# A fixed order of issue for the attention front of a lightning-attention and low-rank mixer kernel, with weight conversion in smaller steps

## Chip, cores and metric

The kernel runs on one core of one Trainium2 chip. The metric is the device time of one execution in microseconds (us). All runs told here fell in the fast state and gave correct results. TensorE is the matrix engine; VectorE (DVE), ScalarE (ACT) and GpSimd (POOL) are the others that compute; SyncE (SP) issues most transfers. PEld in a profile is TensorE loading weights. The *granted clock* is the share of full speed at which TensorE was let run; "half clock" means that its instructions take about twice their usual time.

## The reference, cut to what matters

```python
# attention: B, H, S, D = 4, 8, 768, 64; blocks of 64 along S, with a decay lam per head
for b in range(nb):
    intra = einsum(einsum(qb, kb) * Dmask, vb)
    inter = einsum(qb * lam_pow, kv_state)
    out[block] = intra + inter
    kv_state = lam_block * kv_state + einsum(kb * rev_pow, vb)
x = out.transpose(0, 2, 1, 3).reshape(B, S, 512)
# mixer: U 768x32, V 32x768, w_ch1 512x2048, w_ch2 2048x512
h  = x.transpose(0, 2, 1) @ U @ V
u  = x + h.transpose(0, 2, 1)
out = u + relu(u @ w_ch1) @ w_ch2
```

U, V, w_ch1 and w_ch2 reach the kernel as 64-bit floats. It has to convert them itself.

## The kernel before

The program has two parts. The *front*, about 175 us, does attention in 24 chunks of 128 rows (4 batches of 6 chunks), the low-rank part, and the conversion of U, V and the first blocks of w_ch1. The *feed-forward*, 540 us of matmuls, follows. For each chunk `s` the front runs these pieces:

- `prep`: TensorE transposes q and k (tiles pq, pk), ScalarE copies them out (qt, kt), GpSimd makes scaled ones (qs, ks).
- `scores`: 16 matmuls (pss); VectorE multiplies them by the mask (sm).
- `outputs`: px from sm, v and the state; then the state itself (pkv, kvc, kv).
- `back`: transposes to natural rows (pxn, x_nat).
- `low`, `low_sum`: once per batch, x against U (pp, then pt), summed over four groups (pr), split in two parts (pt_h, p_hl inside vp).
- `mix`, `turn`: x plus the low-rank part (pu, x_nat), transposed and split for the feed-forward (put, ut, u_hl, te, u_d).

```python
def prep(s):
    ...                                   # 8 transposes into pq, pk
    nc.scalar.copy(qt, pq)
    nc.scalar.copy(kt, pk)
    ...                                   # GpSimd: ks, qs

def low(b, chunks):                       # called with chunks 0..4, later with chunk 5
    if 0 in chunks:
        pts[b] = bank([P, C], "pp")
    pp = pts[b]
    for c in chunks:
        g = c % G                         # G = 4 groups of 32 columns of the array
        nc.tensor.matmul(out=pp[g * R : (g + 1) * R, :], lhsT=u_w[:, c, :],
                         rhs=xs[b * NT + c], start=(c < G), stop=(c + G >= NT))
    if NT - 1 in chunks:
        pts[b] = tmp("pt")
        nc.scalar.copy(pts[b], pp)

# order of the pieces
pieces = [("prep", 0), ("scores", 0)]
for s in range(NS):
    b, c = divmod(s, NT)
    step = [("prep", s + 1)] * (s + 1 < NS)
    if b > 0:
        if c > 0:
            step += [("mix", s - NT - 1)]
        else:
            step += [("mix", s - NT - 1)] * (b > 1) + [("low_b", b - 1)]
    step += [("outputs", s)]
    step += [("scores", s + 1)] * (s + 1 < NS)
    step += [("low_a", b)] * (c == NT - 1)
    step += [("low_sum", b - 1)] * (c == 0 and b > 0)
    step += [("back", s)]
    ...                                   # turn
```

A converted weight takes these steps, hung on chunks by number:

```python
fetch  # the words, by SyncE
one    # DVE sc, DVE m; then ScalarE twice over sc
two    # DVE m, DVE sc, DVE wf (the 32-bit weight)
three  # DVE wt; ScalarE w[0]; DVE wl; ScalarE w[1]; DVE w[2]   (the split)

for steps, at in (
    (u_side, (0, 1, 1)), (v_steps(0), (0, 2, 2, 3)), (v_steps(1), (1, 4, 4, 5)),
    (w1_steps(0), (3, 8, 9, 10)), (w1_steps(1), (10, 14, 15, 16)),
): ...
```

The third block of w_ch1, `w1_steps(2)`, belongs to the code *after* the front. In the kernel before, a scheduler decides the order of everything on each engine.

Of the kernel before, what the change touches and what calls it, by code (L numbers as in the profile page):

```python
# [18 lines left out]
def kernel(  # L19
# [76 lines left out]
    def weight_steps(dst, src, n):  # L96

        st = {}
        dims = "p (c f) -> p c f" if len(src.shape) == 3 else None

        def shape(t, f):
            return t.rearrange(dims, f=f) if dims else t

        def fetch():
            if src.dtype == FP32:
                nc.sync.dma_start(out=shape(dst(), src.shape[-1]), in_=src)
                return
            words_pool.append(words_pool.pop(0))
            words = words_pool[-1].tile([P, 2 * C], U32, tag="words", name="words")[:, 0 : 2 * n]
            s = src.bitcast(U32)  # L110
            nc.sync.dma_start(out=shape(words, s.shape[-1]), in_=s)
            st["w"] = words.rearrange("p (n two) -> p n two", two=2)

        def one():
            if src.dtype == FP32:
                return
            hi = st["w"][:, :, 1]
            st["sc"] = sc = wconv.tile([P, C], U32, tag="sc", name="sc")[:, 0:n]
            st["m"] = m = wconv.tile([P, C], U32, tag="m", name="m")[:, 0:n]
            sc_f = sc.bitcast(FP32)  # L120
            nc.vector.tensor_scalar(sc, hi, 20, 0x7FF, ALU.logical_shift_right, ALU.bitwise_and)
            nc.vector.tensor_scalar(m, hi, 0xFFFFF, 0x100000, ALU.bitwise_and, ALU.bitwise_or)

            nc.scalar.activation(out=sc_f, in_=sc, func=AF.Relu, bias=ends[-1][:, 0:1], scale=-1.0)
            nc.scalar.activation(
                out=sc, in_=sc_f, func=AF.Relu, bias=ends[-1][:, 1:2], scale=-float(1 << 23)
            )

        def two():
            if src.dtype == FP32:  # L130
                return
            lo, hi = st["w"][:, :, 0], st["w"][:, :, 1]
            sc, m = st["sc"], st["m"]
            m_f, sc_f = m.bitcast(FP32), sc.bitcast(FP32)
            nc.vector.scalar_tensor_tensor(m_f, lo, 2.0**-32, m, ALU.mult, ALU.add)
            nc.vector.scalar_tensor_tensor(sc, hi, 0x80000000, sc, ALU.bitwise_and, ALU.bitwise_or)
            nc.vector.scalar_tensor_tensor(dst(), m_f, 2.0**-20, sc_f, ALU.mult, ALU.mult)

        return [fetch, one, two]

    def split_steps(tile_of, src):

        st = {}

        def dst():
            if "w" not in st:
                st["w"] = wconv.tile([P, C], FP32, tag="wf", name="wf")
            return st["w"]

        def three():  # L150
            w, t, low = st["w"], tmp("wt"), tmp("wl")
            o = tile_of()
            nc.vector.tensor_scalar(t.bitcast(U32), w.bitcast(U32), HI, None, ALU.bitwise_and)
            nc.scalar.copy(o[:, 0, :], t)
            nc.vector.tensor_tensor(out=low, in0=w, in1=t, op=ALU.subtract)
            nc.scalar.mul(o[:, 1, :], low, 4096.0)
            nc.vector.scalar_tensor_tensor(o[:, 2, :], t, -E, low, ALU.mult, ALU.add)

        return weight_steps(dst, src, C) + [three]

    w1v, w2v = {}, {}

# [18 lines left out]
    def bank(shape, name):  # L181
        return ps.tile(shape, FP32, tag="bank", name=name)
# [2 lines left out]

    raw = {}

    def load(name, s):
        b, c = divmod(s, NT)
        t = raw_pool.tile(  # L190
            [P, H, D], FP32, tag=f"{name}raw", bufs=3, name=f"{name}raw"
        )
        source = {"q": q, "k": k, "v": v}[name]
        nc.sync.dma_start(
            out=t, in_=source[b, :, c * P : (c + 1) * P, :].rearrange("h p d -> p h d")
        )
        raw[s, name] = t
# [36 lines left out]
        nc.vector.tensor_copy(out=rev, in_=mask[:, :, :, P - 1])  # L234
        nc.gpsimd.memset(kv, 0.0)

    def more_constants():
        nc.vector.memset(zeros, 0.0)
        for x in range(2):
            nc.vector.tensor_copy(  # L240
                out=lamh[x * D : (x + 1) * D, :], in_=lamb[x * D : (x + 1) * D, x::2]
            )
        for a in range(HP):
            nc.vector.tensor_tensor_scan(
                powq[:, a, :], lamh[:, a : a + 1].broadcast_to([P, P]),
                zeros.broadcast_to([P, P]), 1.0, ALU.mult, ALU.add,
            )
        grid = ident.rearrange("p (g r) -> p r g", r=R)
        nc.vector.tensor_reduce(out=gather[:, 0, :], in_=grid, axis=mybir.AxisListType.X, op=ALU.add)
        for g in range(1, G):  # L250
            nc.vector.tensor_copy(out=gather[:, g, :], in_=gather[:, 0, :])
# [108 lines left out]

    pts = {}

    def low(b, chunks):

        if 0 in chunks:
            pts[b] = bank([P, C], "pp")
        pp = pts[b]
        for c in chunks:
            g = c % G
            nc.tensor.matmul(  # L370
                out=pp[g * R : (g + 1) * R, :], lhsT=u_w[:, c, :], rhs=xs[b * NT + c],
                start=(c < G), stop=(c + G >= NT),
            )
        if NT - 1 in chunks:
            pts[b] = tmp("pt")
            nc.scalar.copy(pts[b], pp)

    def low_sum(b):
        pr = bank([P, C], "pr")
# [56 lines left out]
    for s in range(NS):  # L436
        b, c = divmod(s, NT)
        step = [("prep", s + 1)] * (s + 1 < NS)
        if b > 0:
            if c > 0:  # L440
                step += [("mix", s - NT - 1)]
            else:
                step += [("mix", s - NT - 1)] * (b > 1) + [("low_b", b - 1)]
        step += [("outputs", s)]
        step += [("scores", s + 1)] * (s + 1 < NS)
        step += [("low_a", b)] * (c == NT - 1)
        step += [("low_sum", b - 1)] * (c == 0 and b > 0)
        step += [("back", s)]
        done = s - NT - 1
        if done >= 0 and done // TG < FG:  # L450
# [1 line left out]
        pieces += step  # L452
    waiting = {name: list(range(NS)) for name in "qkv"}

    def load_next(name):
        if waiting[name]:
            load(name, waiting[name].pop(0))


    run = {  # L460
        "prep": prep, "scores": scores, "outputs": outputs, "back": back,
        "low_a": lambda b: low(b, range(NT - 1)), "low_b": lambda b: low(b, [NT - 1]),
        "low_sum": low_sum, "mix": mix, "turn": turn,
    }
    def v_steps(half):
        cols = slice(half * SH, (half + 1) * SH)
# [4 lines left out]
                st["v"] = tmp("vf")[:, 0:SH]  # L471
            return st["v"]

        def three():
            vf, t = st["v"], tmp("vt")[:, 0:SH]
            nc.vector.tensor_scalar(t.bitcast(U32), vf.bitcast(U32), HI, None, ALU.bitwise_and)
            for g in range(G):
                rows = slice(g * R, (g + 1) * R)
                if g % 2 == 0:
                    nc.scalar.copy(v_hl[rows, cols], t[rows])  # L480
                else:
                    nc.vector.tensor_tensor(
                        out=v_hl[rows, cols], in0=vf[rows], in1=t[rows], op=ALU.subtract
                    )

        return weight_steps(dst, moe_V[:, cols].unsqueeze(0).broadcast_to([G, R, SH]), SH) + [three]


    u_side = weight_steps(
        lambda: u_w.rearrange("p c r -> p (c r)"), moe_U.rearrange("(c p) r -> p c r", p=P), NT * R  # L490
    )
    side = {}
    for steps, at in (
        (u_side, (0, 1, 1)),
        (v_steps(0), (0, 2, 2, 3)),
        (v_steps(1), (1, 4, 4, 5)),
        (w1_steps(0), (3, 8, 9, 10)),
        (w1_steps(1), (10, 14, 15, 16)),
    ):
        for step, n in zip(steps, at):  # L500
            side.setdefault(n, []).append(step)

    load_next("q")
    nc.sync.dma_start(out=lamb, in_=lam.unsqueeze(0).broadcast_to([P, H]))
    load_next("k")
    load_next("v")
    for name in "qkv":
        load_next(name)
    constants()
    for i, (what, s) in enumerate(pieces):  # L510
        run[what](s)
        if i == 1:
            for name in "qkv":
                load_next(name)
            more_constants()
        if what == "scores":
            for step in side.pop(s - 1, ()):
                step()
    assert not side
    att_ctx.close()  # L520
    words_pool[:] = [wconv]

# [68 lines left out]
    def run_units(units, side, every=lambda i: None):  # L591
# [6 lines left out]

    c0, b = NS - NT, B - 1
    rest = [  # L600
        (0, 0, "mix", c0 - 1), (0, 1, "turn", c0 - 2), (0, 5, "low_b", b), (0, 10, "low_sum", b),
        (0, 18, "mix", c0), (1, 0, "turn", c0 - 1), (1, 2, "mix", c0 + 1), (1, 8, "turn", c0),
        (1, 12, "mix", c0 + 2), (1, 16, "turn", c0 + 1), (1, 20, "mix", c0 + 3),
        (2, 0, "turn", c0 + 2), (2, 4, "mix", c0 + 4), (2, 8, "turn", c0 + 3),
# [49 lines left out]
    us = {}  # L654
    acc = {}

    def product(i, n):
        g, ft = steps[i]
        m, hl, dd = ms[i], w2hl[ft // 4][:, ft % 4], w2dd[ft // 4][:, ft % 4]
        if ft == 0:  # L660
# [1 line left out]
        pz, pd = acc[n]  # L662
        cols = slice(n * P, (n + 1) * P)
        first, end = ft == 0, ft == FT - 1
        nc.tensor.matmul(out=pz, lhsT=m[:, 0, cols], rhs=hl[:, 0], start=first, stop=False)  # L665
        nc.tensor.matmul(out=pz, lhsT=m[:, 1, cols], rhs=hl[:, 1], start=False, stop=end)  # L666
        nc.tensor.matmul(out=pd, lhsT=m[:, 2, cols], rhs=dd, start=first, stop=end)  # L667

    def residual(g):

# [54 lines left out]
            for n in range(TG):  # L725
                finish(g, n)
    for n in range(TG):
        for i in range(len(steps) - STAG, len(steps)):
            product(i, n)
        finish(NG - 1, n)  # L730


# [28 lines left out]
```

## Time and profile before

| | before |
|---|---|
| time, median of 3 runs | 717.14 us (716.25 to 717.36) |
| span of the profiled execution | 714.7 us |
| TensorE busy | 97% |
| scores of chunk 23 start at | 156.6 us |
| from there to the end | 558.1 us |

The span is shorter than the time by about 2 us in every run. The starts of pss are the front's clock: a full chunk without waits takes 5.58 us, and whatever lies above that is a wait, a slower clock, or the low-rank part. A *beat* is the time from one chunk's start to the next.

Two places are not shown in the prediction and are needed later. The first is the end of the program. VectorE's timeline of the kernel before (start, length, engine, line, operation, tiles, shapes, count, and idle time with its releaser in brackets):

```profile
710.06 0.69 DVE L682 SCALAR_TENSOR_TENSOR o<-pz,u 128x512 f32<-128x512 f32 x1 [0.63 <-PE pz L666]
710.86 0.69 DVE L685 SCALAR_TENSOR_TENSOR o<-pd,o 128x512 f32<-128x512 f32 x1
```

TensorE's last matmul starts at 709.79, and VectorE ends 1.76 us after that start.

The second is the low-rank product at the second boundary of batches, in TensorE's timeline of the kernel before:

```profile
87.05 1.90 PE L370 MATMUL pp<-x_nat,u_w 128*32 128x512 f32 x10
91.01 1.04 PE L370 MATMUL pp<-x_nat,u_w 128*32 128x512 f32 x2
```

Ten passes (five chunks, two passes each) cost 1.90 us, and the two passes of the sixth chunk, issued apart, cost 1.04 us more.

### The profile page before, as it was taken

The page shows a single profiled execution, that of the slowest core. Times are in us where ns is not written, and L with a number is a line of the kernel's source. Part 1 is how long each engine was busy: PE and PEld are TensorE (multiplying, and loading weights), DVE is VectorE, ACT ScalarE, POOL GpSimd, SP SyncE. Part 2 cuts the span into 40 slices and gives each one's busy share as a digit, 9 for nine tenths or more (in the row PEclk, how much of TensorE's full clock was granted, in tenths as well). Part 3 has the DMA queues.
Part 4 walks back from the last instruction along what each step waited for, and adds up shares of the span by engine and source line. Part 5 has one row for each costly group of instructions (what it writes and reads, how often), then busy time and mean ns, then how long its engine had stood idle before and what let it go on. Part 6 is the DMA issues. An engine that isn't in the chain of part 4 may idle for free.

```text
span 714.7 us, 11406 instructions
## 1 busy us (share of the span) xinstructions
PE 695.1 (97%) x4176; PEld 561.0 (78%) x4176; DVE 506.4 (71%) x909; ACT 309.3 (43%) x543; POOL 110.5 (15%) x91
## 2 busy tenths in 40 slices
PE   6889999999999999999999999999999999999997
PEld 5768788796888888888888888888888888888885
DVE  4676868676899976667779525678677686775864
ACT  3566677575566544454546412223232232222320
POOL 3224455443300000000000000003030030300300
PEclk9999999999999999999999999999999999999999
DMA  9687967513477655565556799965335363363431
GB/s 191 143 191 162 226 153 176 148 61 133 163 242 262 230 206 208 198 214 193 191 213 244 272 326 310 383 216 200 103 119 192 89 206 103 118 188 92 163 90 59
DMA packets 131808, 131.77 MB, mean 184 GB/s; under 512 B 81320, under 2 KB 89512, under 8 KB 131752
## 3 DMA queue, kind: packets, MB, share of 16 engines
q1 hardware_dynamic: 131752, 131.04, 59.1%
q8 instruction: 33, 0.54, 0.3%
q14 instruction: 23, 0.19, 0.1%
HBM read 80.68 MB, written 50.33 MB: 183 GB/s over the span
## 4 chain that ended last, share of the span: by engine, by line
PE 90%; DVE 4%; DMA 4%; ACT 1%; issue 1%; SPq 0%; DVEq 0%; ACTq 0%
PE pz L546 25%; PE pz L666 13%; PE pz L665 13%; PE pd L553 13%; PE pd L667 13%; PE pss L293 3%; DMA words<-in_moe_V_dram 3%; PE px L316 2%; PE px L311 2%; PE pp L370 2%; PE pxn L356 1%; PE put L411 1%; PE pkv L332 1%; PE pk L263 1%; PE pq L263 1%; DMA words<-in_moe_w_ch_dram 1%
## 5 line engine op out<-in xcount | busy, mean ns | idle before, releaser
L546 PE MATMUL pz<-u_hl,w 128*128 128x512 f32 x768 | 190.0, 398 | 0.0
L546 PEld LDWEIGHTS pz<-u_hl,w 128*128 128x128 f32 x768 | 144.2, 188 | 35.9 <-issue 1.3
L667 PE MATMUL pd<-w_d,m 128*128 128x512 f32 x384 | 152.2, 396 | 0.0
L665 PE MATMUL pz<-w_hl,m 128*128 128x512 f32 x384 | 152.2, 396 | 0.0
L666 PE MATMUL pz<-w_hl,m 128*128 128x512 f32 x384 | 152.2, 396 | 0.0
L650 ACT ACTIVATE m<-mt 128x512 fp32r<-128x512 f32 x96 | 60.7, 632 | 192.2 <-PE pd L667 145.0
L651 DVE SCALAR_TENSOR_TENSOR m<-rm,m 128x512 fp32r<-128x512 f32 x96 | 71.5, 746 | 49.4 <-ACT m L650 49.1
L561 DVE SCALAR_TENSOR_TENSOR r<-pd,r 128x512 f32<-128x512 f32 x96 | 61.9, 685 | 59.0 <-ACT r L560 51.0
L687 POOL TENSOR_TENSOR o<-o,u 128x512 f32<-128x512 f32 x20 | 29.8, 1521 | 449.9 <-DVE o L685 449.9
L553 PE MATMUL pd<-u_d,w 128*128 128x512 f32 x384 | 98.4, 397 | 0.0
L560 ACT ACTIVATE r<-pz 128x512 f32<-128x512 f32 x96 | 52.3, 596 | 99.4 <-PE pz L546 99.4
L666 PEld LDWEIGHTS pz<-w_hl,m 128*128 128x128 f32 x384 | 72.3, 188 | 17.6
L667 PEld LDWEIGHTS pd<-w_d,m 128*128 128x128 f32 x384 | 72.3, 188 | 17.6
L665 PEld LDWEIGHTS pz<-w_hl,m 128*128 128x128 f32 x384 | 72.3, 188 | 17.6
L553 PEld LDWEIGHTS pd<-u_d,w 128*128 128x128 f32 x384 | 72.1, 188 | 17.3
L652 DVE SCALAR_TENSOR_TENSOR m<-m 128x512 fp32r<-128x512 f32 x96 | 68.7, 717 | 0.9
L649 DVE TENSOR_SCALAR mt<-rm 128x512 uint32<-128x512 uint32 x96 | 46.2, 481 | 27.9 <-DMA rm<-r_d 27.6
L316 PE MATMUL px<-sm,vraw 128*64 128x128 f32 x384 | 41.3, 285 | 3.5 <-DVE sm L299 3.4
L311 PE MATMUL px<-qs,kv 128*64 128x128 f32 x320 | 37.2, 285 | 1.5 <-issue 1.5
L316 PEld LDWEIGHTS px<-sm,vraw 128*64 128x64 f32 x384 | 29.7, 143 | 8.6 <-DVE sm L299 5.7
L299 DVE TENSOR_TENSOR sm<-pss,mask 128x512 f32<-128x512 f32 x48 | 30.9, 684 | 7.3 <-PE pss L293 6.1
L280 POOL TENSOR_TENSOR qs<-qt,powq 128x512 f32<-128x512 f32 x20 | 26.5, 1324 | 55.5 <-ACT qt L267 55.5
(81 smaller groups left out, 774.2 us busy)
## 6 DMA issues: line engine op xcount, KB each, us to landing
r_d<-r SPq DMA_DIRECT2D x96, 256.0 KB, 2.1
rm<-r_d SPq DMA_DIRECT2D x96, 256.0 KB, 2.7
words<-in_moe_w_ch_dram SPq DMA_DIRECT2D x32, 512.0 KB, 4.1
w_d<-w SPq DMA_DIRECT2D x16, 768.0 KB, 3.3
w_hl<-w_d SPq DMA_DIRECT2D x16, 512.0 KB, 6.3
qraw<-in_q_dram SPq DMA_DIRECT2D x24, 256.0 KB, 4.1
kraw<-in_k_dram SPq DMA_DIRECT2D x24, 256.0 KB, 4.9
vraw<-in_v_dram SPq DMA_DIRECT2D x24, 256.0 KB, 4.0
```

The source lines that it names most:

```text
L311: nc.tensor.matmul(out=px[rows, a, :], lhsT=kv[:, a, rows], rhs=qs[:, a, :], start=True, stop=False,)
L316: nc.tensor.matmul(out=px[x * D : (x + 1) * D, a, :], lhsT=vr[:, 2 * a + x, :], rhs=sm[:, x, a, :], start=(c == 0), stop=True,)
L546: nc.tensor.matmul(out=acc[g][0], lhsT=w[:, n, ct, :], rhs=uhl[g][:, n, ct, :], start=(ct == 0 and n == 0), stop=(ct == CT - 1 and n == 1),)
L553: nc.tensor.matmul(out=acc[g][1], lhsT=w[:, 2, ct, :], rhs=ud[g][:, ct, :], start=(ct == 0), stop=(ct == CT - 1),)
L560: nc.scalar.mul(r, pz, 1.0 + E)
L561: nc.vector.scalar_tensor_tensor(r, pd, 4096.0, r, ALU.mult, ALU.add)
L650: nc.scalar.activation(out=m[:, 0], in_=t, func=AF.Relu)
L651: nc.vector.scalar_tensor_tensor(m[:, 1], r, 0.0, hi, ALU.max, ALU.subtract)
L652: nc.vector.scalar_tensor_tensor(m[:, 2], hi, E, low, ALU.mult, ALU.subtract)
L665: nc.tensor.matmul(out=pz, lhsT=m[:, 0, cols], rhs=hl[:, 0], start=first, stop=False)
L666: nc.tensor.matmul(out=pz, lhsT=m[:, 1, cols], rhs=hl[:, 1], start=False, stop=end)
L667: nc.tensor.matmul(out=pd, lhsT=m[:, 2, cols], rhs=dd, start=first, stop=end)
```

## The change

The intent: the scheduler lets VectorE start on words that have not landed, while a score product waits. So fix the order of issue for the whole front, cut the conversion into smaller steps at chosen places, and bring the low-rank product together.

```diff
-        return [fetch, one, two]
+        return [fetch, one, two, three]       # two and three: the old two, halved
-    def low(b, chunks):
+    def low(b):
-        for c in chunks:
+        for c in range(NT):
...
+        step += [("mix", s - NT - 1)] * (s > NT)
+        step += [("low", b - 1)] * (c == 0 and b > 0)
         step += [("outputs", s)]
+        step += [("low_sum", b - 1)] * (c == 0 and b > 0)
         step += [("scores", s + 1)] * (s + 1 < NS)
-        step += [("low_a", b)] * (c == NT - 1)
-        step += [("low_sum", b - 1)] * (c == 0 and b > 0)
         step += [("back", s)]
...
-        (u_side, (0, 1, 1)),
-        (v_steps(0), (0, 2, 2, 3)),
-        (v_steps(1), (1, 4, 4, 5)),
-        (w1_steps(0), (3, 8, 9, 10)),
-        (w1_steps(1), (10, 14, 15, 16)),
+        (u_side, (None, -2, 2, 2)),
+        (v_steps(0), (None, -3, 4, 4, 5, 5)),
+        (v_steps(1), (3, -5, 5, 6, 6, -7)),
+        (w1_steps(0), (7, -9, 10, 11, 12)),
+        (w1_steps(1), (9, -14, 15, 16, 17)),
...
+    with tc.manual_schedule():
+        load_next("q")
+        load_next("k", nc.scalar)
+        nc.scalar.dma_start(out=lamb, in_=lam.unsqueeze(0).broadcast_to([P, H]))
+        for name in "vqkvqkv":
+            load_next(name)
+        for step in first:                    # None: words of U and V, ahead of the front
+            step()
+        constants()
+        for i, (what, s) in enumerate(pieces):
+            run[what](s)
...
+            if what == "outputs":
+                for step in early.pop(s, ()): # negative numbers: behind outputs(|n|)
+                    step()
+            if i + 1 == len(pieces) or pieces[i + 1][0] == "prep":
...
+                for step in late.pop(n, ()):  # positive numbers: at the end of chunk n
+                    step()
...
     for n in range(TG):
-        for i in range(len(steps) - STAG, len(steps)):
-            product(i, n)
+        for parts in ((0, 1), (2,)):          # last sums: pz of three steps, then pd
+            for i in range(len(steps) - STAG, len(steps)):
+                product(i, n, parts)
         finish(NG - 1, n)
```

V's steps are now six (the split has two parts). The code behind the front, with `w1_steps(2)`, is still ordered by the scheduler. Line numbers move: pss is L293 before and L302 after, kt L268 and L277, pp L370 and L377.

> **What bounds the kernel now.** I read the page first, then the chain of waits in order of time, then TensorE's timeline for its gaps, and the timelines of the engines that it waited for.
>
> ```profile
> PE 695.1 (97%) x4176; PEld 561.0 (78%) x4176; DVE 506.4 (71%) x909; ACT 309.3 (43%) x543; POOL 110.5 (15%) x91
> ```
>
> TensorE is the bound, and most of that can't move. The two feed-forward products are 1152 + 1152 matmuls of 512 columns (the page's L546, L553, L665, L666, L667), and the chain shows eight of them in 1.87 to 1.88 us, so 0.234 us each and 540 us in all. Of the 714.7 us span, 175 us are left for the attention front, the start and the end. The change works there. The front has 24 chunks, and the starts of their score matmuls (pss) give its beat.
>
> ```profile
> 14.17 1.09 PE pss L293 x16
> 17.65 18.19 DMA words<-in_moe_V_dram x2
> 47.39 1.09 PE pss L293 x16
> 106.65 1.09 PE pss L293 x16
> 112.24 1.14 PE pss L293 x16
> ```
>
> These are lines of the chain: start, length, work. Between 106.65 and 112.24 a chunk takes 5.59 us and TensorE has no gap: the pace of a full chunk. In the first batch, which has no mixing yet, TensorE's timeline has starts at 14.10, 19.02 and 23.93: 4.92 us. But chunks 1 to 6 take 33.2 us (14.17 to 47.39), where five times 4.92 is 24.6. The next view, TensorE's timeline, has the gaps.
>
> ```profile
> 37.15 1.07 PE L316 MATMUL px<-sm,vraw 128*64 128x128 f32 x3 [1.98 <-DVE sm L299]
> 98.24 0.47 PE L394 MATMUL pu<-vp 128*128 128x512 f32 x1 [0.80 <-DVE vp L387]
> 124.75 1.16 PE L293 MATMUL pss<-qt,kt 64*128 64x128 f32 x16 [0.72 <-ACT kt L268]
> ```
>
> The bracket is idle time and who ended it. VectorE's own timeline says why sm was late:
>
> ```profile
> 35.87 0.36 DVE L121 TENSOR_SCALAR sc<-words 128x384 uint32<-128x384 uint32 x1 [2.05 <-DMA words<-in_moe_V_dram]
> 36.14 0.35 DVE L122 TENSOR_SCALAR m<-words 128x384 uint32<-128x384 uint32 x1
> 36.41 1.28 DVE L299 TENSOR_TENSOR sm<-pss,mask 128x512 f32<-128x512 f32 x2
> ```
>
> The masked scores stand in VectorE's queue behind a conversion whose words have not landed.
>
> **What the Trainium skill says.** (1) "TensorE: Matmul & The Clock Gate", the opening table: ScalarE's, VectorE's and GpSimd's queues are strict FIFO. The trace agrees: sm above waited 2.05 us for data that is not its own. So the order of issue alone can cost or win time. (2) The same page, "What's actually happening": the array falls to half clock when idle and comes back after sustained work. The trace agrees: after the 1.98 us gap the granted clock of 35 to 40 us is 0.73. A stall can cost more than its own length. (3) "GPSIMD Engine Reference", Specifications: its SBUF interface is shared with VectorE, with contention for instructions with two SBUF inputs. The trace agrees: wl (two SBUF inputs) takes 1.58 us at both of its places in the front, beside running GpSimd work, against a median of 0.686 over its 32 runs of the same size. (4) "DMA: Bandwidth & Descriptors", "Issuing engines are not separate DMA queues": a second issuing engine saves issue time only. So k0 on ScalarE's queue gains at most its later issue (1.85 instead of 0.74 us), shared with q0's transfer.
>
> **The change, part by part.** I take TensorE's pace without gaps and add the waits that the new order makes.
>
> *Start.* pss of chunk 0 began at 7.97. k0 goes out about 1.1 us sooner, but q0 still needs its four transposes at half clock (1.09 us), then k0's (1.1), then kt (0.59). VectorE used to finish masks, powers and gather before sm, at 10.09; now powers (1.37) and gather (0.34 + 1.23) come later, so it is free. I gain 0.7 us: chunk 1 at 13.4.
>
> *First batch.* Words are fetched early and converted behind the scores. Five beats of 4.92: chunk 6 at 38.0. I add 0.5 for raw loads that now queue behind 0.6 MB of words. Before: 47.3. Gain here 8.8 beyond none, with the start included.
>
> *Low-rank part.* All twelve passes (1.83 + 0.97 = 2.80 us) and the gather product (1.05) now come ahead of the next scores, so their results ripen behind 3.0 us of other TensorE work (1.09 + 0.58 + 0.44 + 0.88), where 1.5 are needed. A batch's boundary of two chunks becomes 8.56 + 5.58 = 14.14 us; before it took 15.05 twice. Gain 0.9 at each before new waits. At the first boundary 7.9 + 5.3 = 13.2 against 14.1.
>
> *Two chunks each at 72.6 to 86.0 and 112.2 to 124.75.* These lose 1.2 + 1.5 and 1.9 us today to words and to conversion in front of sm. Without waits they take 5.58 and, for a last chunk without state, 5.12.
>
> *Sum without new waits:* 13.4 + 24.6 + 13.2 + 3 x 5.58 + 5.12 + 14.14 + 3 x 5.58 + 5.12 + 14.14 + 3 x 5.58 = 139.9 us for the start of chunk 23's scores, against 156.6 now: 16.7 us of gain at most.
>
> *New waits.* The fixed order puts ScalarE's two writes of a converted weight ahead of the next chunk's qt and kt, where the scheduler had slipped kt in front. These are lines of before for one such conversion, VectorE's and ScalarE's:
>
> ```profile
> 117.22 1.58 DVE L155 TENSOR_TENSOR wl<-wf,wt 128x512 f32<-128x512 f32 x1
> 116.55 0.57 ACT L268 COPY kt<-pk 128x512 f32<-128x512 f32 x1
> 118.83 0.63 ACT L156 ACTIVATE w<-wl 128x512 fp32r<-128x512 f32 x1 [0.58 <-DVE wl L155]
> ```
>
> There ScalarE waits for wl after kt; in the new order kt waits with it. At the second boundary, from the end of the gather product: VectorE does pt_h and p_hl (1.45), sm (1.25), ut and u_hl (1.4), wt (0.5), wl (1.58): 6.2. Then ScalarE's w (0.63) and qt, kt (1.05): 7.9. TensorE wants kt at 5.6 (one beat). Wait 2.3 us. By the same count at the third boundary (no pt_h, one step of another weight between, then the copy pt): 7.85 against 6.42, 1.4 us. At chunk 8, V's second half: vf at 1.5, its writes, then kt: 0.9 to 1.8, I take 1.3. The two opening steps add 1.45 us of ScalarE work (two of 0.72) ahead of kt, which has about 1.05 of room in a beat: 0.4 each. With the 0.5 of the loads: 6.3 us.
>
> *End.* The last pz sum now ends three matmuls before pd, so L682 (0.69) runs beside pd, instead of between 710.06 and 710.86: about 0.5 us off. Nothing else in the 540 us moves.
>
> Total: 16.7 - 6.3 + 0.5 = 10.9, so 706.2. Some of the counted waits may not fall so badly, since VectorE's contention is the largest guess in them, so I say 705.5.
>
> **The rivals.** *All waits gone:* the steps fit in VectorE's and ScalarE's slack, wl is not slowed. For it: a beat without conversion leaves VectorE 1.37 us idle before kvc. Against it: wl took 1.58 both times. Time: 717.1 - 17.2 = 699.9. *ScalarE becomes the wait:* as I count, with the 2.3 us gap bringing half clock again as at 37 us, 1.7 us more: about 708. *Loads become the wait:* the transfers ran full from 5 to 20 us (218 GB/s); words of U and V put ahead of chunks 3 and 4's q and k could delay them by their 0.6 MB, 2.7 us. Up to chunk 3's q and k there are eleven pieces of 0.262 MB and 0.59 MB of words, 3.47 MB in all; with 0.58 MB moved in the first 5 us (116 GB/s) and 218 to 223 GB/s after it, they are in by about 18.2, wanted at about 19: thin. If they miss: 2 us more and perhaps half clock, 708 to 710. *The scheduler was better:* a fixed order that blocks at every chunk would give back everything, 715 or more; the unchanged beat of 5.58, which the scheduler reached with the same order of scores, output and state, speaks against it.
>
> **Range and chances.** The ends are 699.9 (no new wait) and about 710 (mine plus clock and loads). 2% faster means under 702.8, a gain of 14.3 out of 17.2 possible: new waits would have to stay under 2.9 us, where I count 6.3. I give that 0.3, within 2% 0.67, slower 0.03. Range 700.0 to 710.5.
>
> **What would show it.** Right: pss starts 4.92 apart from chunk 1 to 6, no wait of VectorE for words, chunk 6 near 38; low-rank boundaries without pu waiting for vp; TensorE's longest gap at chunk 14's pss, waiting for ScalarE's kt, about 2.3 us, with wl at 1.58 and w ahead of kt; smaller ones at chunks 8 and 19; L682 of the last rows ended before the last matmul. Wrong: q or k as releaser of TensorE at 18 to 25 us, wl at 0.7 us, kt never a releaser, or a beat other than 5.58 in chunks without conversion.

## The result

| | before | after |
|---|---|---|
| time, median of 4 runs | 717.05 us (716.25 to 717.36) | 712.22 us (711.04 to 713.1) |
| span of the profiled execution | 714.7 us | 710.8 us |
| scores of chunk 23 start at | 156.6 us | 153.4 us |
| from there to the end | 558.1 us | 557.4 us |

The ratio is 0.9933, 95% interval 0.9916 to 0.9951. Ratios here are the mean time of one kernel's fast runs over that of the other's fast runs of the same rounds, so not quite the ratio of the medians that are quoted. The change is faster by 0.7%, which counts as "within 2%". The predicted 705.5 us was 6.7 us too low; the range had ended at 710.5.

Part 1 of the page after, with busy time by engine:

```profile
PE 690.2 (97%) x4176; PEld 560.0 (79%) x4176; DVE 508.2 (71%) x909; ACT 308.5 (43%) x543; POOL 109.9 (15%) x91
```

The number of instructions per engine is the same as before, so only their order and grouping differ. Next, TensorE's timeline of the kernel after, cut to the larger gaps and what follows the largest:

```profile
21.31 0.66 PE L272 MATMUL pq<-ident,qraw 128*128 128x128 f32 x4 [0.70 <-DMA qraw<-in_q_dram]
22.51 0.63 PE L272 MATMUL pk<-ident,kraw 128*128 128x128 f32 x4 [0.55 <-DMA kraw<-in_k_dram]
45.27 1.05 PE L377 MATMUL pp<-x_nat,u_w 128*32 128x512 f32 x2 [1.07 <-ACT x_nat L367]
55.52 1.16 PE L302 MATMUL pss<-qt,kt 64*128 64x128 f32 x16 [1.37 <-ACT kt L277]
73.80 1.16 PE L302 MATMUL pss<-qt,kt 64*128 64x128 f32 x16 [0.54 <-ACT kt L277]
93.72 1.16 PE L302 MATMUL pss<-qt,kt 64*128 64x128 f32 x16 [1.38 <-ACT kt L277]
106.13 1.16 PE L302 MATMUL pss<-qt,kt 64*128 64x128 f32 x16 [0.53 <-ACT kt L277]
127.11 2.07 PE L386 MATMUL pr<-pt,gather 128*128 128x512 f32 x2 [3.48 <-DVE kvc L348]
129.11 2.08 PE L302 MATMUL pss<-qt,kt 64*128 64x128 f32 x16
```

TensorE's 1.98 us wait for sm of the kernel before is gone. In its place stand waits for ScalarE's kt, foreseen, and one of 3.48 us at the third boundary of batches, not foreseen in this size. The two lines at the end take about twice their usual 1.13 and 1.16 us: half clock.

The starts of pss give a ledger by stretch of chunks. "Predicted" adds up the prediction's terms for the stretch. The last two columns are two experiments told below.

| stretch | predicted | after | third weight fixed | best |
|---|---|---|---|---|
| start to chunk 1 | 13.4 | 13.9 | 13.9 | 12.4 |
| 1 to 6 | 25.1 | 25.8 | 25.9 | 24.9 |
| 6 to 8 (first boundary, V) | 14.5 | 15.8 | 15.8 | 13.1 |
| 8 to 12 | 22.3 | 23.6 | 23.6 | 24.2 |
| 12 to 14 (second boundary) | 16.4 | 14.6 | 14.6 | 13.3 |
| 14 to 18 | 22.3 | 23.3 | 23.3 | 23.6 |
| 18 to 20 (third boundary) | 15.5 | 19.6 | 14.1 | 13.3 |
| 20 to 23 | 16.7 | 16.8 | 18.0 | 18.4 |
| chunk 23 starts at | 146.2 | 153.4 | 149.0 | 143.2 |

Each column is one execution. The changed kernel's second profiled execution (told below) took 12.6, 29.9 and 13.6 us in the first three stretches, 56.1 us in all where the first took 55.5, and agreed within 0.1 us from chunk 8 on; so the split of the first three rows is loose.

The kernel after misses the prediction by 7.1 us at chunk 23, and 4.1 of them lie in one stretch, from 18 to 20. Four views of the kernel after show that place. First VectorE's timeline:

```profile
119.61 0.67 DVE L421 TENSOR_SCALAR ut<-put 128x512 uint32<-128x512 uint32 x1
120.70 0.43 DVE L121 TENSOR_SCALAR sc<-words 128x512 uint32<-128x512 uint32 x1 [0.42 <-DMA words<-in_moe_w_ch_dram]
121.05 0.68 DVE L431 TENSOR_TENSOR u_hl<-put,ut 128x512 fp32r<-128x512 f32 x1
121.98 1.51 DVE L122 TENSOR_SCALAR m<-words 128x512 uint32<-128x512 uint32 x1
123.41 1.54 DVE L162 TENSOR_TENSOR wl<-wf,wt 128x512 f32<-128x512 f32 x1
```

L121 and L122 here are step `one` of the *third* weight. They come from the code behind the front, and the scheduler has put them into VectorE's queue inside the fixed stretch, between the instructions of chunk 18 (ut and u_hl are the turn of chunk 11, which is done there). L121 waits for words, u_hl waits behind it, and L122 and wl take 1.51 and 1.54 us, where 0.42 and 0.69 are their usual lengths (L122 took 1.50 us at 68.30 and at 100.64 too). The chain of waits of the kernel after runs through the transfer of those words:

```profile
116.14 4.46 DMA words<-in_moe_w_ch_dram
```

Then ScalarE's timeline:

```profile
124.98 0.63 ACT L163 ACTIVATE w<-wl 128x512 fp32r<-128x512 f32 x1 [2.27 <-DVE wl L162]
125.98 0.59 ACT L277 COPY kt<-pk 128x512 f32<-128x512 f32 x1
126.46 0.60 ACT L382 COPY pt<-pp 128x512 f32<-128x512 f32 x1
```

ScalarE idles 2.27 us for wl, and only after that write come qt, kt and pt. pr needs pt, which ends at 127.06; TensorE starts it at 127.11. (The bracket of pr names kvc, which ended at 127.09, only 0.03 us after pt. But pr does not need it: in the run with the third weight placed by hand, told below, pr starts at 124.33, after pt's end at 124.28 and before kvc starts at 124.37.) Last the table by windows, with busy us and instructions of PE, PEld, DVE, ACT, POOL, then TensorE's granted clock, DMA share and GB/s:

```profile
120.00:125.00 5.00, 3.63 (x46) 1.81 (x44) 4.58 (x7) 1.79 (x4) 2.53 (x2) 1.00 0.89 208
125.00:130.00 5.00, 2.89 (x10) 1.39 (x12) 2.83 (x6) 3.28 (x8) 1.27 (x1) 0.64 0.66 157
130.00:135.00 5.00, 5.00 (x43) 4.53 (x43) 3.77 (x6) 2.30 (x5) 0.00 (x0) 0.68 0.03 9
```

The clock falls to 0.64 and 0.68 in the two windows. Between 130 and 135 TensorE is busy all the time and gets through 43 instructions.

The places that went better than predicted: at the second boundary wl took its normal time, and the twelve low-rank passes together took less. VectorE's and then TensorE's timeline of the kernel after:

```profile
91.35 0.69 DVE L162 TENSOR_TENSOR wl<-wf,wt 128x512 f32<-128x512 f32 x1 [0.16 <-ACT te L433]
```

```profile
82.30 1.91 PE L377 MATMUL pp<-x_nat,u_w 128*32 128x512 f32 x12
```

Twelve passes cost 1.91 us, against 1.90 + 1.04 for ten and two. The prediction had carried the old sum over.

### The profile page after: what moved, and what is told of

The parts are those of the page before. It is cut to its first block, busy times and chain, and to the rows that moved or that the text cites. A ratio compares the mean times of both kernels' runs of the same rounds, so it can differ in the third digit from the quotient of the medians.

```text
span 710.8 us, 11432 instructions
## 1 busy us (share of the span) xinstructions
PE 690.2 (97%) x4176; PEld 560.0 (79%) x4176; DVE 508.2 (71%) x909; ACT 308.5 (43%) x543; POOL 109.9 (15%) x91
## 4 chain that ended last, share of the span: by engine, by line
PE 89%; DMA 4%; DVE 4%; ACT 2%; issue 1%; SPq 0%; DVEq 0%; ACTq 0%
PE pz L561 25%; PE pz L683 13%; PE pz L681 13%; PE pd L568 13%; PE pd L685 13%; PE pss L302 3%; PE px L325 2%; PE px L320 2%; DMA kraw<-in_k_dram 1%; DMA words<-in_moe_V_dram 1%; PE pxn L365 1%; PE put L417 1%; PE pk L272 1%; PE pq L272 1%; DVE sm L308 1%
## 5 line engine op out<-in xcount | busy, mean ns | idle before, releaser
L325 PE MATMUL px<-sm,vraw 128*64 128x128 f32 x384 | 37.7, 280 | 0.3 <-DVE sm L308 0.3
L302 PE MATMUL pss<-qt,kt 64*128 64x128 f32 x384 | 29.7, 297 | 4.9 <-ACT kt L277 4.7
L302 PEld LDWEIGHTS pss<-qt,kt 64*128 64x128 f32 x384 | 24.9, 199 | 10.5 <-ACT kt L277 6.5
L320 PE MATMUL px<-qs,kv 128*64 128x128 f32 x320 | 32.9, 279 | 0.0
```

What stands on the lines that cost most here:

```text
L302: nc.tensor.matmul(out=pss[x][:, a, :], lhsT=kt[rows, a, :], rhs=qt[rows, a, :], start=True, stop=True,)
L325: nc.tensor.matmul(out=px[x * D : (x + 1) * D, a, :], lhsT=vr[:, 2 * a + x, :], rhs=sm[:, x, a, :], start=(c == 0), stop=True,)
```

## The experiments

The question has two parts: why the third boundary costs 4 us more than reckoned, and what the other parts of the change are worth. For the boundary there were three theories. *Stray steps:* the third weight's steps, which the fixed order does not hold, delay VectorE. *Writes in front:* ScalarE's two writes of a converted weight stand ahead of the next chunk's qt, kt and pt, so TensorE inherits every delay of wl. *Words:* V's and the weights' words come too late, or the chunks' loads do. Experiments are told in the order in which they answer this. "After" names the changed kernel; diffs are against it unless said otherwise. Each ratio is against the kernel before, run on the same chip.

### The third weight's steps placed by hand

```diff
+    third = w1_steps(2)
...
         (w1_steps(1), (9, -14, 15, 16, 17)),
+        (third[:3], (12, -20, 23)),
...
-    run_units([(pairs[2], 0), (pairs[2], 1)], w1_steps(2))
+    run_units([(pairs[2], 0), (pairs[2], 1)], third[3:])
```

> The changed kernel, with the third weight's fetch and first two steps given fixed places (chunks 12, 20 and 23) instead of being lifted by the scheduler into chunk 18; its last steps stay where the feed-forward part had them, so that part is not starved as it was with everything fixed. Theory C (the stray steps make the 3.48 us wait and the half clock behind it): as in the front of the all-fixed run, the wait at the third boundary is near 0.7 us, no half clock, and now the whole kernel gains it: about 5 us, 707 to 708 us. Rival (what the front gains, the feed-forward part loses to the later third and fourth weight): no better than the changed kernel, 712 us.

Measured: 708.49 us (707.96 to 708.98), ratio 0.9893 (0.988 to 0.9907), span 707.1. TensorE's timeline and two windows of this run, at the third boundary:

```profile
124.33 1.13 PE L386 MATMUL pr<-pt,gather 128*128 128x512 f32 x2 [0.72 <-ACT pt L382]
```

```profile
120.00:125.00 5.00, 4.28 (x48) 2.11 (x46) 4.55 (x7) 4.43 (x9) 3.48 (x3) 1.00 0.89 207
125.00:130.00 5.00, 5.00 (x61) 4.25 (x61) 4.41 (x7) 2.96 (x7) 1.00 (x1) 1.00 0.80 191
```

With the stray steps elsewhere wl takes 0.69 us and ends at 122.16 instead of 124.95; pr waits 0.72 us, not 3.48, and the clock stays at 1.00. The stretch from 18 to 20 takes 14.1 us, not 19.6, and the stretches before it stay as they were (ledger, the column of this run). Later a kt wait of 0.53 us appears, and 1.2 us of the gain go in chunks 20 to 23. The stray steps are shown as the cause of the large miss: 3.7 us of span, and 3.7 us of the median time.

### The writes of the weights one chunk later

```diff
-            nc.scalar.copy(o[:, 0, :], t)          # out of step four
-            nc.scalar.mul(o[:, 1, :], low, 4096.0)
+        def writes():                              # a step of its own
+            nc.scalar.copy(o[:, 0, :], t)
+            nc.scalar.mul(o[:, 1, :], low, 4096.0)
...
-        (w1_steps(0), (7, -9, 10, 11, 12)),
-        (w1_steps(1), (9, -14, 15, 16, 17)),
+        (w1_steps(0, True), (7, -9, 10, 11, 12, -13)),
+        (w1_steps(1, True), (9, -14, 15, 16, 17, -18)),
```

> The changed kernel with one thing undone: ScalarE's two writes of a converted weight (w1 of step 0 and 1) are issued one chunk later, behind the next qt, kt (and pt). Theory A (ScalarE's fixed order is what costs: kt and pt wait behind w, which waits for VectorE's wl): the 1.38 us wait for kt at 93.7 us and the 3.48 us wait at 127.1 us shrink to under 1.5 us together, the half clock after the second one is gone, about 706 us. Rival B (VectorE is behind at these places anyway, ScalarE only passes its delay on): the waits move to the scores' sm or to pu and the time stays within 2 us of the changed kernel, 710 to 712 us.

Measured: 708.74 us (708.39 to 709.13), ratio 0.989 (0.9869 to 0.9911), span 706.6. TensorE's timeline of this run at the third boundary, with the stray steps still in VectorE's queue:

```profile
122.64 1.12 PE L397 MATMUL pr<-pt,gather 128*128 128x512 f32 x2
126.73 0.63 PE L428 MATMUL put<-ident,x_nat 128*128 128x128 f32 x4 [1.30 <-DVE x_nat L414]
129.49 0.49 PE L411 MATMUL pu<-vp 128*128 128x512 f32 x1 [1.25 <-ACT vp L403]
```

VectorE is as late as in the kernel after: L122 takes 1.51, wl 1.54 us. But pt is now ahead of the writes on ScalarE, and pr has no wait. VectorE's delay reaches TensorE later and in two parts, 2.55 us in all, without half clock. So it took both for the large loss: the stray steps made wl late, and the write in front of kt and pt passed that on in one piece, with half clock behind it. The stretch from 18 to 20 takes 19.6 us with both, 16.5 with the stray steps alone, 14.1 with the writes in front alone, and 13.7 with neither (the next run).

### Both, with V's writes later too

```diff
+    third = w1_steps(2)                            # and third[:3] at (12, -20, 23), as above
-        (v_steps(0), (None, -3, 4, 4, 5, 5)),
-        (v_steps(1), (3, -5, 5, 6, 6, -7)),
+        (v_steps(0), (None, -3, 4, 4, 5, -6, -6)), # V's ScalarE writes a step of their own
+        (v_steps(1), (3, -5, 5, 6, 6, -7, -7)),
+        (w1_steps(0, True), (7, -9, 10, 11, 12, -13)),
+        (w1_steps(1, True), (9, -14, 15, 16, 17, -18)),
```

> The run with the third weight at fixed places (708.5 us), with ScalarE's writes of V's halves and of the two weights issued behind the next chunk's qt and kt. Theory A: the waits for kt at 55.5 and 93.7 us (1.37 + 1.38 us) and the 0.72 us for pt at 124.3 go; about 1.2 us come back as new waits for kt one chunk later (writes are 1.24 us, room about 0.65): 1.5 to 2.5 us faster, 706.5 us. Rival B (VectorE's backlog is the limit): 708 us or more, waits for sm, x_nat or pu in their place.

Measured: 708.43 us (707.83 to 709.47), ratio 0.9893 (0.9878 to 0.9909). It is no faster than either alone. The kt waits at 55.5 and 93.7 us and the pr wait are gone, but new ones stand at 61.95 (0.54 us) and 100.24 (1.17 us), one chunk later, as the expectation had reckoned (writes of 1.24 us, room for about 0.65). In the profiled execution q also came 2.01 us late at 21.4 us; it came 2.08 late in the run with late writes alone, and 0.74 in the one with the third weight alone. So part of the gain may be hidden by that late load. But moving the writes as a block did move the waits.

### Everything fixed, up to the first feed-forward units

```diff
+    with tc.manual_schedule():
         for i, (pair, ft) in enumerate([(pairs[0], 0), (pairs[1], 0), (pairs[0], 1), (pairs[1], 1)]):
             ...
         run_units([(pairs[2], 0), (pairs[2], 1)], w1_steps(2))
```

> The changed kernel with the first twelve feed-forward units in a fixed order too, so that the scheduler can no longer lift the third weight's first steps (L121, L122, L133) into VectorE's queue at chunk 18. Theory C (these stray steps, their wait for words and the contended 1.5 us ones make the third boundary's wait): the 3.48 us wait falls to about 1.4 us, too short for half clock, so about 5 us are won: 707 us. Rival A alone (kt and pt behind w and wl, stray steps or not): the wait stays at 2.5 us or more with half clock behind it, 711 us or more. The fixed units themselves may cost or win 1 us.

Measured: 720.22 us (719.84 to 720.86), ratio 1.0049 (1.0031 to 1.0067), span 719.0. TensorE's timeline of this run:

```profile
124.95 1.13 PE L386 MATMUL pr<-pt,gather 128*128 128x512 f32 x2 [0.72 <-ACT pt L382]
206.21 6.48 PE L561 MATMUL pz<-u_hl,w 128*128 128x512 f32 x16 [6.95 <-ACT w L161]
```

The front did what the stray-steps theory says: pr waits 0.72 us and chunk 23 starts at 148.4. But the third weight was then fetched and converted only where the code has it, and the feed-forward stood still for 6.95 us, with half clock behind it (6.48 us for 16 matmuls that take 3.91 elsewhere). The stray steps were not an error of the scheduler as such: it had filled a need that the fixed order did not know.

### The low-rank part alone, in the kernel before

Against the kernel before:

```diff
-                step += [("mix", s - NT - 1)] * (b > 1) + [("low_b", b - 1)]
+                step += [("mix", s - NT - 1)] * (b > 1) + [("low", b - 1)]   # all six chunks
-        step += [("low_a", b)] * (c == NT - 1)
```

> The kernel before with one part of the change alone: all six chunks of the low-rank product issued together, the scheduler's order otherwise. In the trace after, the twelve passes took 1.84 us (82.4 to 84.2) where the five and the one took 1.83 + 0.97 us. Theory D (issued together, chunks 4 and 5 run side by side in other columns of the array): 0.95 us less in each of four batches, 3.5 to 4 us faster than before, about 713.3 us. Rival: the passes cost the same and only the place differs: within 1 us of before, 717 us.

Measured: 713.75 us (712.81 to 714.55), ratio 0.9957 (0.9937 to 0.9978), span 711.0. Chunk 23 starts at 153.1 instead of 156.6. TensorE's timeline:

```profile
87.64 1.91 PE L368 MATMUL pp<-x_nat,u_w 128*32 128x512 f32 x12
```

Here, too, twelve passes take 1.91 us. Chunks 4 and 5 use two different groups of array columns (0 and 1); the passes of chunk 5 add nothing when they are issued beside those of chunk 4, and 1.0 us when they are issued apart. At four boundaries this is 4 x 1.0 us at most. The profiled span falls by 3.7, about as much as for the whole change (3.9); but this was the fastest of the four runs. By the means of all runs of the same rounds, the low-rank part alone is worth 2.9 us and the whole change 4.8 and 4.5 us (two rounds), with intervals that overlap. So this small part gives about two thirds of the gain. In the kernel after, the passes stayed apart at the first boundary (ten, then two, at 45.27 above).

### The last sums alone, in the kernel before

```diff
-        for i in range(len(steps) - STAG, len(steps)):
-            product(i, n)
+        for parts in ((0, 1), (2,)):
+            for i in range(len(steps) - STAG, len(steps)):
+                product(i, n, parts)
```

> The kernel before with the last sums' order alone: VectorE's next to last instruction runs beside the last three matmuls. Theory: 0.45 to 0.5 us less, 716.5 us against 717.0, the end of VectorE's last instruction 1.3 us after the last matmul's start instead of 1.76. Rival: nothing, hidden by the last transfer.

Measured: 716.21 us (714.25 to 717.86, 6 runs), ratio 1.0003 (0.9987 to 1.0019). Half a microsecond is below what these runs resolve. The trace of this run shows the mechanism all the same, VectorE ending 1.28 us after the last matmul's start, and so does that of the kernel after. VectorE's timeline of the kernel after, at its end:

```profile
706.19 0.69 DVE L700 SCALAR_TENSOR_TENSOR o<-pz,u 128x512 f32<-128x512 f32 x1 [0.61 <-PE pz L683]
706.99 0.69 DVE L703 SCALAR_TENSOR_TENSOR o<-pd,o 128x512 f32<-128x512 f32 x1
```

VectorE ends 1.29 us after TensorE's last matmul starts (at about 706.4), where the kernel before needed 1.76. L700 begins before that last start, but does not end before it.

### The first k back on SyncE's queue

```diff
-        load_next("k", nc.scalar)
-        nc.scalar.dma_start(out=lamb, in_=lam.unsqueeze(0).broadcast_to([P, H]))
+        nc.sync.dma_start(out=lamb, in_=lam.unsqueeze(0).broadcast_to([P, H]))
+        load_next("k")
```

> The changed kernel with the first k load and lambda back on SyncE's queue, in the order of before. Theory: q0 lands at 4.0 instead of 4.8 us and lambda at 4.4 instead of 6.7, k0 later; scores of chunk 0 begin within 0.5 us of the changed kernel's 7.38; the time is within 0.6 us of the changed kernel's. Rival: the early k0 is worth its 1.1 us, this run is 1 us slower.

Measured: 710.54 us (709.67 to 712.2, 6 runs), ratio 0.9921 (0.9907 to 0.9936); the interval overlaps that of the kernel after. q's transposes start at 3.96 instead of 4.77 us, and the first scores at 7.71 instead of 7.38: what k gains, q loses. This part is worth nothing that can be measured. TensorE's timeline of this run has something else to note:

```profile
21.63 0.66 PE L272 MATMUL pq<-ident,qraw 128*128 128x128 f32 x4 [1.18 <-DMA qraw<-in_q_dram]
22.82 0.64 PE L272 MATMUL pk<-ident,kraw 128*128 128x128 f32 x4 [0.54 <-DMA kraw<-in_k_dram]
23.88 0.64 PE L325 MATMUL px<-sm,vraw 128*64 128x128 f32 x4
```

From 23.4 us on px takes 0.64 us instead of 0.39 and the granted clock of 20 to 25 and of 25 to 30 us is 0.83, though no single wait was longer than 1.18 us.

### V's second half later

```diff
-        (v_steps(1), (3, -5, 5, 6, 6, -7)),
+        (v_steps(1), (3, -7, 7, 8, 8, -9)),
```

> The changed kernel with the second half of V converted two chunks later (it is first needed by the fourth mixed chunk), its words fetched at the same place. Theory E (VectorE's 3.76 us wait for V's words at 43.1 us delays x_nat, pt and then kt on ScalarE, and these cost TensorE 1.07 + 1.37 us and the unpacked passes): these waits go, new ones of about 0.5 us come at chunks 8 to 10, 1.5 to 2.5 us faster than the changed kernel, about 710 us. Rival: the wait only moves with the conversion, no gain: 712 us.

This tests the loss at chunks 6 to 8. In the kernel after, VectorE idles 3.76 us at 43.08 for V's words, which were issued at 33.45 and took 9.5 us to land.

Measured: 712.46 us (710.58 to 717.04), ratio 0.9949 (0.991 to 0.9988): no gain. The waits at 45 and 55 us are gone, but chunk 10's scores now wait 3.72 us for kt (at 66.88): on ScalarE the writes of V stand in front of kt, and they waited 2.93 us for VectorE, where two instructions of V's conversion had slowed to 1.66 and 1.03 us. Again the wait was moved and not removed.

### The words of U and V behind the chunks' loads

With the third weight placed as above, and:

```diff
-        (u_side, (None, -2, 2, 2)),
-        (v_steps(0), (None, -3, 4, 4, 5, 5)),
+        (u_side, (0, -3, 3, 3)),
+        (v_steps(0), (1, -4, 4, 4, 5, 5)),
```

> The run with the third weight at fixed places (708.5 us), with the words of U and of V's first half fetched behind the raw loads of chunks 3 and 4 and U's steps one chunk later. Loads theory (words put ahead delay q and k of chunk 3): the waits of 0.7 and 0.55 us for q and k at 21 and 22.5 us go, chunks 1 to 5 start 4.92 us apart, 1.3 to 1.7 us faster: 706.9 us. Rival: the words then come late for their conversion, VectorE waits for them and the scores behind it: no gain, 708.5 us.

Measured: 710.64 us (708.64 to 712.29, 6 runs), ratio 0.9924 (0.9908 to 0.994): slower than with the words in front. The chunks' loads are in time (chunks 1 to 5 start 4.91 us apart), but V's second half now lands later still. VectorE's and TensorE's timelines of this run:

```profile
43.58 0.36 DVE L121 TENSOR_SCALAR sc<-words 128x384 uint32<-128x384 uint32 x1 [5.85 <-DMA words<-in_moe_V_dram]
```

```profile
45.76 1.91 PE L377 MATMUL pp<-x_nat,u_w 128*32 128x512 f32 x2 [3.38 <-ACT x_nat L367]
```

VectorE waits 5.85 us with its queue blocked, TensorE 3.38 us, and the two passes take 1.91 instead of 1.05 us, at half clock. In these two orders, whichever load was put later came late.

### The changed kernel again

> The changed kernel itself again, as the base for the others on this chip: 711 to 713 us, ratio to before 0.992 to 0.995.

Measured: 712.28 us (708.78 to 713.28, 6 runs), ratio 0.9938 (0.9919 to 0.9958). This profiled execution had a wait of 2.35 us for q at 21.61 us, with half clock behind it, where the first one had 0.70 and none; the kernel before had no wait for q after the start. So the change also brought a load that comes just in time or just too late, and the spread of 4.5 us is wider than that of the other variants but one.

### All small mends at once

The third weight placed; each ScalarE write (and the second ScalarE pass of step `one`) a step of its own, nearly always one per chunk, behind that chunk's `outputs`; the words behind the loads, and V's steps spread:

```diff
+        (u_side, (0, -3, 3, 3)),
+        (v_steps(0), (1, -4, 5, 5, 5, -6, -6)),
+        (v_steps(1), (3, -6, 6, 6, 6, -7, -7)),
+        (w1_steps(0, True), (7, -9, -10, 10, 11, 12, -13, -14)),
+        (w1_steps(1, True), (9, -15, -16, 16, 17, 18, -19, -19)),
+        (third[:4], (12, -20, -21, 23)),
```

> All mends in one: the third weight in fixed places; ScalarE's writes of V and of the weights one chunk later and one at a time, its two opening writes in two chunks; the words of U and V behind the raw loads of chunks 3 and 4. Theories A, C and the loads theory together: no wait of TensorE over 1 us in the front after the start, scores of chunk 23 begin near 142 to 144 us, 701 to 703 us, over 2% faster than before. Rival (VectorE's backlog with GpSimd's contention sets these places, whatever ScalarE does): waits for sm, pu or x_nat of 1 us and more remain at the boundaries, 705 us or more.

Measured: 707.14 us (705.29 to 707.6), ratio 0.987 (0.9854 to 0.9886), span 705.6. The expected gain was missed: six waits of 0.5 to 1.2 us remained, five for kt and one for vp.

### Step one behind the turn

As the last one, but step `one` goes from behind `outputs` to the end of the chunk, behind u_hl:

```diff
-        (v_steps(0), (1, -4, 5, 5, 5, -6, -6)),
-        (w1_steps(0, True), (7, -9, -10, 10, 11, 12, -13, -14)),
-        (w1_steps(1, True), (9, -15, -16, 16, 17, 18, -19, -19)),
-        (third[:4], (12, -20, -21, 23)),
+        (v_steps(0), (1, -4, 4, 4, 5, -6, -6)),
+        (w1_steps(0, True), (7, 9, -10, 10, 11, 12, -13, -14)),
+        (w1_steps(1, True), (9, 15, -16, 16, 17, 18, -19, -20)),
+        (third[:4], (12, 21, -22, 23)),
-                if n == 3:
+                if n == 1:
                     make_gather()
```

> An attempt at the best version: the all-mended run (707.1 us), with the opening step of each weight moved from in front of the scores to behind u_hl, its second ScalarE write one chunk later, and gather made at chunk 1. Expected: the waits of 0.53 to 1.18 us for kt at chunks 9, 11, 15, 17 and 21 fall to 0.1 each, 3 us less: 703.5 to 704.5 us. Rival (ScalarE then has both steps ahead of kt in the same chunk): no better than 707 us.

Measured: **702.76 us** (702.47 to 703.76, 4 runs), ratio 0.9816 (0.9801 to 0.9831), span 700.8. It beats both kernels: 13.6 us below the 716.31 us (median) of the kernel before in its rounds. The larger gaps left in TensorE's timeline after the first scores, up to chunk 23:

```profile
47.49 0.51 PE L419 MATMUL pu<-vp 128*128 128x512 f32 x1 [0.61 <-ACT vp L411]
57.83 1.16 PE L321 MATMUL pss<-qt,kt 64*128 64x128 f32 x16 [0.54 <-ACT kt L296]
94.73 1.16 PE L321 MATMUL pss<-qt,kt 64*128 64x128 f32 x16 [0.65 <-ACT kt L296]
131.65 1.16 PE L321 MATMUL pss<-qt,kt 64*128 64x128 f32 x16 [0.67 <-ACT kt L296]
```

None is longer than 0.7 us, and after the start the clock does not drop in the front. Chunk 23 starts at 143.2, 10.2 us sooner than in the kernel after. In this trace L122 of the three w_ch1 weights takes 0.42 to 0.43 us, where the run before it had 1.27 to 1.50; but which of the several moves weighs most was not taken apart.

## Why the prediction was wrong

**What held.** The bound and the place were right: everything happened in the front, and TensorE's work did not change. TensorE's waits for sm behind unlanded words, which the reading of the kernel before rested on, went away (though VectorE itself still waited for words, 3.76 us at 43.08), and the new releaser is ScalarE's kt, as counted: 1.37 us at chunk 8 (predicted 1.3). Chunks without conversion keep 5.58 us. The end gained 0.47 us in the trace (predicted 0.5), though L700 overlaps only in part. The sum without waits was near as well: it put chunk 23 at 139.9, and the best order found comes to 143.2, at 702.8 us against the 699.9 us reckoned for none. But it is no exact floor: it carries the twelve passes at 2.80 us where they took 1.91, at three boundaries.

**The step that failed.** It is this one: "By the same count at the third boundary (no pt_h, one step of another weight between, then the copy pt): 7.85 against 6.42, 1.4 us." The wait was 3.48 us, and the half clock behind it cost 2.8 more: pr 2.07 instead of 1.13, and the beat from chunk 19 to 20 7.51 instead of 5.65 us with the third weight fixed. The stray step is in the count ("one step of another weight between"), but as a step without a wait of its own; how much of the 7.85 us it was given is not written out. In fact it brought three costs: it waited 0.42 us for words that could only be fetched once the second weight had freed their buffer (issued at 116.14 us, landed at 120.6); its second instruction took 1.51 us, 1.1 more than usual; and it pushed wl to a moment at which wl took 1.54 (the prediction had 1.58 for wl here, so this last one was not underrated). Besides, TensorE came there 0.9 us sooner than reckoned, as the twelve passes took 1.91 us. Together 0.42, 1.1 and 0.9 us cover the 2.1 us by which the wait was longer. To this comes half clock, which the prediction had kept for a rival. Placing the stray step by hand turned 19.6 us of this stretch into 14.1. So the prediction's mechanism at this place (kt and pt behind the write behind wl) was right, and its size was wrong: 3.48 against 1.4 us for the wait, and 6.3 against 1.4 with the half clock. The cause lies in code outside the fixed stretch. What the prediction gave to a rival, half clock after a longer gap, came at the third boundary and not at the second.

**The smaller terms.** These are measured minus predicted, from the ledger. The start +0.5, chunks 1 to 6 +0.7: loads came 0.70 and 0.55 us late at 21 to 23 us (a rival that was named; I had put 0.5 in for it, and reckoned the loads in by about 18.2 us). Chunks 6 to 8 +1.3: V's words took 9.5 us to land and blocked VectorE, which "no wait of VectorE for words" had excluded. The beats with an opening step +0.8 each (6.8 instead of 5.58, so 1.2 longer, where 0.4 was counted): the kt wait is 0.53 us, near what was thought, but sm comes late in the same beat, behind an L122 of 1.50 us, and stretches px as well. This makes most of the +1.3 from 8 to 12 and the +1.0 from 14 to 18. Against that stands -1.8 at the second boundary: the wait was 1.38 instead of 2.3 us, because wl took 0.69 and not 1.58, and the twelve low-rank passes took 0.93 us less than the old sum. All together, with nothing at chunks 20 to 23: +7.1.

**The estimate of contention.** It was the largest guess, and it failed in both directions: where the prediction had it (wl at the second boundary) it did not come, as u_d started only at 91.39, beside wl, and took the longer time itself (1.78 us); at the third boundary it came twice. GpSimd's timeline of the kernel after, beside the lines of VectorE shown above:

```profile
91.39 1.78 POOL L434 TENSOR_TENSOR u_d<-te,u_hl 128x512 fp32r<-128x512 f32 x1 [4.00 <-ACT te L433]
121.87 1.33 POOL L434 TENSOR_TENSOR u_d<-te,u_hl 128x512 fp32r<-128x512 f32 x1 [3.06 <-DVE u_hl L431]
123.17 1.23 POOL L281 TENSOR_TENSOR ks<-kraw,small 128x512 f32<-128x512 f32 x1
```

In these three pairs the one that started first kept about its usual length, and the other took longer: wl (91.35) before u_d (91.39), u_d (121.87) before L122 (121.98), ks (123.17) before wl (123.41). In the kernel before, too, u_d had started first where wl took 1.58 us (79.45 and 79.98; 116.79 and 117.22). So far as these pairs show, the 1.58 us belonged to an order of starts, and the prediction carried it over to the second boundary, where that order turned round.

**What the parts are worth.** By themselves: the low-rank passes together 2.9 us by the means of all runs (3.7 us of one span); the last sums about 0.5, not resolved in time; the first k on ScalarE's queue nothing, as the prediction's reading of its fourth citation had allowed ("at most its later issue"). The fixed order with its conversion steps is worth little as written, and much when it is finished: with the third weight in it 708.5, with the writes spread and step `one` moved 702.8 us.

**Still open.** Whether q's wait at 21 us is 0.7 or 2.4 us changes from execution to execution of one kernel, and what decides it was not found. Nor was the last gain, from 707.1 to 702.8 us, taken apart.

## What to carry to other kernels

When you fix an order by hand, every instruction that may fall into the stretch must be placed, also those of later code: the scheduler fills the gaps of your order with them, and a short instruction that waits for a transfer (here 0.42 us), or takes three times its usual length (1.51 us), holds up what stands behind it in the queue. On an in-order engine put work that nobody waits for (here ScalarE's weight writes) behind the next chunk's copies that somebody does wait for, and in pieces smaller than the room of one beat; moved in one block it moved part of the wait. Take apart a bundle of changes: here one regrouped product of twelve matmuls was worth about two thirds of the whole.

## What the Trainium skill lacked or had wrong

- "TensorE: Matmul & The Clock Gate", "HAM oscillation — how this bites in real kernels", gives idle gaps of more than about 3.4 us as those to avoid. In these runs the clock also halved after single gaps of 1.87 us (the last sums alone, at 28.6 us), 1.98 us (kernel before), 2.08 us (writes later; pq took 1.10 us) and 2.35 us (the changed kernel again; pq 1.12 us), and after gaps of 1.18 and 0.54 us close together (the first k back on SyncE's queue). It did not after 2.01 us (both writes later; pq 0.66 us), 2.09 us (everything fixed) or 2.10 us (the low-rank part alone). So gaps well under 3.4 us can be followed by half clock, the length of one gap alone does not decide it, and no threshold is shown here.
- "GPSIMD Engine Reference", Specifications, names the contention with VectorE's instructions in a 2-port performance mode or with two SBUF inputs (SBUF is the on-chip memory), without a size; the skill has more on it elsewhere, so this is no lack of the whole. The sizes here: VectorE's L122, L142 and wl took 1.50 to 1.73 us where 0.42 to 0.69 is usual, and GpSimd's u_d 1.78 where 1.27 is usual.
- No page has the landing time of a transfer behind a backlog: in the kernel after, 384-column words of V took 9.5 us from issue in a queue with other loads ahead of them (33.45 us), and the 512-column words of a later weight 4.5 us (116.14 us).
